# Slot attention and a GELU network on one core: the written order of the first 490 pieces is changed

## The chip, the core and the metric

The kernel runs on one core of a Trainium2 chip. The metric is the device time of one execution in microseconds (us); the number given for a kernel is the median of three runs. PE is the matrix engine (PEld its weight loads), DVE, ACT and POOL are the three engines that work on vectors, and SP only issues transfers (DMA).

## What is computed

```python
a = exp(phi - max(phi, 2));  a = a / (sum(a, 2) + 1e-9)       # softmax over the sequence of 576
k_m, v_m = einsum(a, k), einsum(a, v)                         # 32 slots of 64 per batch and head
scores = q @ k_m.T / 8                                        # 8 batches, 8 heads, 576 x 32
attn = softmax(scores)                                        # over the 32 slots
x = (attn @ v_m).transpose(0, 2, 1, 3).reshape(4608, 512)
h = x @ w_in                                                  # w_in 512 x 2048
g = 0.5 * h * (1 + erf(h / sqrt(2)))
out = g @ w_out                                               # w_out 2048 x 512
```

`w_in` and `w_out` come as 64-bit floats, taken as pairs of 32-bit integers, and are decoded on the chip. Every product is made from a high and a low part of its operands (hi*hi + hi*lo + lo*hi) in the format fp32r.

## The kernel before

The program is one list of **pieces**, small functions such as `h.0.3.1`, that are called one after the other. Each engine gets its instructions in the order of this list and works through them strictly in that order; an instruction starts when its turn has come and its operands and its place in memory are there. Engines run apart from each other and meet only in such waits. The first 1044 pieces stand in a string `START` (line 53 on), which sets their order by hand; what comes later is put in order by due times. A second string, `HOME`, says which buffer each tile uses; a piece that writes into a buffer waits until the last reader of what was in it is done. An ending `:a` or `:d` on a copying piece says that ACT or DVE makes the copy.

The first pieces are the start of everything and so have little to hide behind. They are, with the lines that stand in the profile:

- `Lphi`, `Lkv0`, `Lkv`, `Lq`, `Lwi.f`, `Lwo.f` (lines 372, 412/413, 396, 420/427, 300): transfers of phi, of keys and values, of queries, and of 512 KB each of `w_in` and `w_out`, for f = 0 to 15. All go through SP's one queue.
- Decoding of one half f.k (k = 0 is `w_in`, k = 1 is `w_out`): `dB` two instructions on ACT (lines 321 and 322), `dC`, `dG`, `dS` on DVE (lines 326, 330, 334), then an addition on POOL, `dDi.f` for `w_in` (line 356, out `w_in`) or `dDo.f` for `w_out` (line 356, out `y`). `dE.f` (line 246, out `wo`) and `dF.f` (line 362) split `w_out` into its high and low part.
- Softmax of phi and slots: `amax` (440, DVE), `aexp` (446, ACT), `anorm` (453), `at` (471, PE, transposes, tile pt), `atc` (246, ACT, copies to aT), `slots` (575, PE, tile pk), `km` (593), `slotsT` (604, PE, tile tn), `kT` (246). For batch 0 the keys come first and the values half a stage later, so `slots.0.g.0`, `slotsT.0.0`, `kT.0.0` are the keys and `slots.0.g.1`, `slotsT.0.1`, `kT.0.1` the values.
- Scores of batch 0: `ns.0`, `ns.1` (633, PE, tile psc), `nc` (246, copies sc), `n_score.x` (679, PE), and on DVE and ACT `n_max`, `n_sub`, `n_exp`, `n_sum`, `n_inv`, `n_mul` (698 to 718), for three parts x; back through PE with `n_T.x` (738, tile pT), and split by `n_hi` (753, ACT) and `n_lo` (757, DVE) into p_hi and p_lo. `n_hi.2` and `n_lo.2` hold the last 64 columns, from `n_T.2`. Batch 1 does the same in a whole with `score.1.hf` (633), `sT` (776), `max`, `sub`, `exp`, `sum`, `inv`, `mul`, `pT` (820), `ph`, `pl` for each half hf.
- `Up.b.f.n` (633, PE, tile pu) multiplies the values' slots by `w_in`; `Uh` and `Ul` (246 and 934) split it. It needs the decoded `w_in` f.
- `h.b.f.hf` (979, PE): six matmuls, hi by p_hi, hi by p_lo, lo by p_hi. `gelu.b.f.hf` (1003, 1005, 1006, ACT), `gh` (246) and `gl` (1012, DVE) give the two parts of g.
- `p.b.f` (1025, PE, tile acc): four times three matmuls, gh by wo_hi, gh by wo_lo, gl by wo_hi. Eight steps f of batch 0 are followed by eight of batch 1, then eight and eight again; `o` empties acc after each eight.
- `W` (346): matmuls of ones whose result nobody reads.

On PSUM there are eight banks: four for acc (used before that by the transposes and scores of batch 0), two that h alternates between, and a pair called `at`, with one generation at a time. `pt`, `pk`, `tn`, `psc` and `pu` all take this pair in turn, so each of them waits until the last one has been copied out.

Of the kernel before, what the change touches and what calls it, by code (L numbers as in the profile page):

```python
# [59 lines left out]
Lwi.2 W.3.246 W.3.245 W.3.244 W.3.243 W.3.242 W.3.241 W.3.240 slots.0.0.1 n_sub.1 aexp.1.0  # L60
Lkv.1.0.1 dS.0.0 dE.0:a dS.1.0 dG.0.0 Lkv.1.0.2 W.3.249 W.3.248 W.3.247 slots.0.1.1 dDi.1
km.0.0.1 n_exp.1 Lkv.1.0.4 n_sum.0 amax.1.1 W.3.29 km.0.1.1 Lkv.1.1.2 dDi.0 n_sum.1 aexp.1.1
slotsT.0.1 Lkv.1.1.1 n_inv.0 kT.0.1 Lwi.4 dB.3.1 n_max.2 n_mul.0 W.3.455 W.3.454 W.3.453
W.3.452 W.3.451 W.3.450 Up.0.0.1 dF.0 Uh.0.0:a W.3.456 n_T.0 Lkv.1.0.3 Ul.0.0 dB.2.1 n_inv.1
Up.0.1.1 Lq.1.0 n_mul.1 Uh.0.1:a dC.2.1 Lwi.3 dB.2.0 n_T.1 Ul.0.1 Lkv.1.1.0 dS.2.1 n_sub.2
at.1.0.0 dG.2.1 n_exp.2 n_hi.0 at.1.1.0 dC.2.0 dDo.2 atc.1.0.0:a n_sum.2 n_lo.0 h.0.0.0
atc.1.1.0 n_inv.2 dE.2:a dS.2.0 n_mul.2 n_hi.1 at.1.1.4 at.1.0.4 dG.2.0 n_T.2 atc.1.1.4
atc.1.0.4:a n_hi.2 slots.1.0 dC.3.1 dDi.2 anorm.1 Lkv.1.1.3 n_lo.1 Lkv.1.1.4 n_lo.2 h.0.0.1
gelu.0.0.0 Lphi.2.0 dS.3.1 km.1.0 dG.3.1 Lwo.4 Up.0.2.1 gelu.0.0.1 Lwi.5 dF.2 dB.3.0 dDo.3
h.0.1.0 Lwo.7 Uh.0.2:d Lwo.5 Ul.0.2 h.0.1.1 gh.0.0:a Lphi.2.1 dC.3.0 Lwi.7 slots.1.1 gelu.0.1.1  # L70
gl.0.0 Lwi.6 gelu.0.1.0 dG.3.0 dE.3 h.0.2.0 km.1.1 dS.3.0 gh.0.1:a amax.2.0 dDi.3 dB.4.0
slotsT.1 h.0.2.1 kT.1:d dF.3 dB.4.1 Up.0.3.1 dC.4.0 dG.4.0 p.0.0 Uh.0.3 dB.5.0 gl.0.1 Ul.0.3
gelu.0.2.1 dG.5.0 gelu.0.2.0 dB.5.1 dC.4.1 dS.4.0 score.1.0 dC.5.0 dDi.4 h.0.3.0 Lq.1.1
sT.1.0.1 sT.1.0.0 Lwo.6 h.0.3.1 dS.5.0 dG.4.1 dDi.5 Up.0.4.1 gelu.0.3.1 max.1.0 p.0.1 Uh.0.4:a
gelu.0.3.0 Ul.0.4 sub.1.0 dS.4.1 dC.5.1 exp.1.0 dDo.4 gh.0.2:a sum.1.0 Up.0.5.1 dG.5.1 h.0.4.0
Uh.0.5:a dE.4 gl.0.2 h.0.4.1 gh.0.3:a Ul.0.5 dS.5.1 p.0.2 dF.4 dDo.5 inv.1.0 gelu.0.4.1
amax.2.1 dB.6.0 dC.6.0 mul.1.0 gelu.0.4.0 dE.5 score.1.1 gl.0.3 dB.6.1 h.0.5.0 dS.6.0 dF.5
# [1629 lines left out]
```

## Time and profile before

| | |
|---|---|
| median of three runs | 688.5 us (687.85 to 688.77) |
| the profiled execution: device time | 688.54 us |
| the profiled execution: span of the trace | 686.8 us |
| busy share of the span: PE, PEld, DVE, ACT, POOL | 98%, 85%, 67%, 58%, 7% |
| PE busy | 675.6 us |

The device time is 1.7 us longer than the span of the trace, and 0.04 us from the median. Times below are us from the span's start. In a timeline a row has the start, how long it took, the engine, the line, the operation with out<-in, shapes and count, and in brackets the idle time of this engine just ahead of it and what ended that. Rows of equal instructions are merged.

### The profile page before, as it was taken

To read this page: it belongs to the slowest core of one execution; us is meant where nothing else is said; L and a number is where in the kernel's file an instruction comes from. 1 tells how busy PE (TensorE), PEld (TensorE's weight loads), DVE (VectorE), ACT (ScalarE), POOL (GpSimd) and SP (SyncE) were. 2 spreads that over 40 slices of the span, in tenths; PEclk is the share of its full clock that TensorE was granted. 3 is DMA by queue.
4 is the path that set the end of the run, shared out by engine and by line. 5 is a ranking of instruction groups with operands and counts; after the bars stand their busy time and mean duration, and the time that the engine had idled before them with its cause. 6 is when DMAs were issued, how large, how long until landed. Compare 5 with 4: busy or idle time off the path is not lost.

```text
span 686.8 us, 13988 instructions
## 1 busy us (share of the span) xinstructions
PE 675.6 (98%) x5440; PEld 583.8 (85%) x5440; DVE 463.0 (67%) x912; ACT 396.4 (58%) x977; POOL 45.6 (7%) x38
## 2 busy tenths in 40 slices
...
GB/s 336 368 305 89 122 211 102 82 108 196 54 193 208 175 177 165 67 177 191 266 49 31 154 107 333 284 280 411 64 150 161 66 1 154 158 31 1 33 1 61
DMA packets 54173, 105.11 MB, mean 153 GB/s; under 512 B 5724, under 2 KB 23900, under 8 KB 52572
## 3 DMA queue, kind: packets, MB, share of 16 engines
...
q8 instruction: 43, 0.70, 0.4%
...
## 4 chain that ended last, share of the span: by engine, by line
PE 89%; DMA 4%; DVE 3%; ACT 2%; issue 1%; SPq 0%; DVEq 0%; ACTq 0%
PE acc L1025 31%; PE h L979 28%; PE m L1270 19%; PE pu L633 4%; PE tacc L1025 3%; DMA kv<-kv 1%; DMA raw<-w_in 1%; PE psc L633 1%; PE psc L550 1%; DMA phi<-phiT 1%; DMA q<-qT 1%; DMA raw<-w_out 1%; PE x L550 1%; PE pk L550 0%; DVE gl L1012 0%
## 5 line engine op out<-in xcount | busy, mean ns | idle before, releaser
L979 PE MATMUL h<-p_hi,U 128*128 128x288 f32 x1024 | 203.8, 298 | 0.3 <-ACT p_hi L753 0.3
L1025 PE MATMUL acc<-wo,gh 128*128 128x512 f32 x640 | 198.9, 392 | 0.0
L979 PEld LDWEIGHTS h<-p_hi,U 128*128 128x128 f32 x1024 | 160.9, 188 | 19.4 <-issue 6.0
L1025 PEld LDWEIGHTS acc<-wo,gh 128*128 128x128 f32 x640 | 116.0, 188 | 25.5 <-issue 1.2
L1025 PE MATMUL acc<-wo,gl 128*128 128x512 f32 x320 | 125.1, 391 | 0.2 <-DVE gl L1012 0.2
L979 PE MATMUL h<-p_lo,U 128*128 128x288 f32 x512 | 109.2, 295 | 0.2 <-DVE p_lo L757 0.2
L1212 ACT CAST hi<-x 128x384 fp32r<-128x384 f32 x108 | 61.3, 568 | 37.1 <-DVE x L1205 34.0
L979 PEld LDWEIGHTS h<-p_lo,U 128*128 128x128 f32 x512 | 81.4, 188 | 0.5 <-DVE p_lo L757 0.5
L1270 PE MATMUL m<-wo,hi 128*128 128x256 f32 (+1 forms) x378 | 81.5, 298 | 0.2 <-DVE o L1300 0.2
L997 ACT ACTIVATE gf<-h 128x256 f32<-128x256 f32 x96 | 36.9, 387 | 76.5 <-PE h L979 52.0
L1012 DVE TENSOR_TENSOR gl<-gf,gh 128x512 fp32r<-128x512 f32 x80 | 57.0, 714 | 30.0 <-ACT gh L246 27.5
L1216 DVE TENSOR_TENSOR lo<-x,hi 128x384 fp32r<-128x384 f32 x108 | 67.1, 622 | 12.3 <-ACT hi L1212 12.1
L994 ACT ACTIVATE x<-h 128x256 f32<-128x256 f32 x96 | 36.9, 385 | 63.5 <-PE h L979 63.5
L1025 PEld LDWEIGHTS acc<-wo,gl 128*128 128x128 f32 x320 | 60.1, 188 | 14.1 <-DVE gl L1012 1.1
L1270 PE MATMUL m<-sum,hi 128*128 128x256 f32 x324 | 62.5, 282 | 0.0
L1270 PEld LDWEIGHTS m<-wo,hi 128*128 128x128 f32 x378 | 60.3, 190 | 2.6 <-DVE o L1300 0.5
L1201 DVE TENSOR_TENSOR x<-x 128x256 f32<-128x256 f32 x56 | 23.8, 424 | 57.2 <-ACT x L994 57.2
L1270 PE MATMUL m<-wo,lo 128*128 128x256 f32 x216 | 60.9, 282 | 0.0
L1270 PEld LDWEIGHTS m<-sum,hi 128*128 128x128 f32 x324 | 50.4, 190 | 0.2
L1270 PE MATMUL m<-sum,lo 128*128 128x256 f32 x162 | 45.5, 281 | 0.0
L934 DVE TENSOR_TENSOR U<-pu,U 128x512 fp32r<-128x512 f32 (+2 forms) x38 | 30.8, 827 | 20.9 <-ACT U L246 20.8
L1270 PEld LDWEIGHTS m<-wo,lo 128*128 128x128 f32 x216 | 41.0, 190 | 0.0
...
## 6 DMA issues: line engine op xcount, KB each, us to landing
...
```

The costliest lines, as they stand in the source:

```text
L550: nc.tensor.matmul(pk[32 * j : 32 * j + 32, : 2 * D], st["aT", b][:, c, g, 32 * j : 32 * j + 32], st["kv", b, g, c][:, :, j, :], start=(c ...
L633: nc.tensor.matmul(ps[g][M * j : M * j + M], st["kT", b][rows, t, M * j : M * j + M], moving[j][rows], start=True, stop=True,)
L934: nc.vector.tensor_sub(u[:, ..., 1, :], pu, u[:, ..., 0, :].bitcast(F32))
L979: i = nc.tensor.matmul(h[:, :HS], u[g][w], x[:, g, :], start=(n == 0), stop=(n == 3 * G - 1))
L994: nc.scalar.activation(x, h.rearrange("p (a n) -> p a n", a=2), AF.Gelu)
L997: nc.scalar.activation(gf[:, f % 2 * n : f % 2 * n + n], h, AF.Gelu)
L1012: nc.vector.tensor_tensor(g_of("gl", *k), g_of("gf", *k), g_of("gh", *k).bitcast(F32), op=ALU.subtract)
L1025: nc.tensor.matmul(acc, x, w[:, f, :], start=(first and n == 0), stop=(last and n == 2))
L1201: nc.vector.tensor_tensor(x[:, 5:7], x[:, 1:2].to_broadcast([P, 2, P]), x[:, 0:3:2], op=ALU.subtract)
L1212: nc.scalar.copy(split_of("hi", b, hf, i, part), source(b, hf, i, part))
L1216: nc.vector.tensor_tensor(lo, source(b, hf, i, part), hi.bitcast(F32), op=ALU.subtract)
L1270: nc.tensor.matmul(d, x, y, start=(i == 0 and k == 0 and bank not in seen), stop=(i == NP - 1 and k == len(three) - 1), skip_group_check=True,
```

## The change

Only `START` differs. It holds the same 1044 pieces in both kernels. The order differs up to piece 489; right after it comes `h.0.8.0`, where batch 0's second half begins after eight steps of batch 0 and eight of batch 1, and from there on the lists are the same. 13 copies get another engine: `dE.1`, `kT.1`, `gh.0.6`, `ph.1.1`, `gh.1.2`, `gh.1.3`, `gh.1.4` go from DVE to ACT; `dE.0`, `o.0.0.7`, `gh.1.0`, `gh.1.1`, `gh.1.5`, `dE.11` from ACT to DVE. `aexp.2.1` and `aexp.2.0`, which stood on both sides of `exp.1.1`, stand together much later, after `gh.1.5`; ACT's list therefore has two more loads of a function table (40 instead of 38).

```diff
-Lwo.1 Lphi.0.1 Lphi.0.0 Lkv0.0.0 Lkv0.1.0 Lwo.0 dB.1.1 Lq.0.0 amax.0.1 Lq.0.1 aexp.0.1 amax.0.0
-dC.1.1 dG.1.1 aexp.0.0 anorm.0 at.0.0.0 dS.1.1 dDo.1 at.0.1.0 atc.0.0.0:a at.0.0.4 at.0.1.4
...
+Lphi.0.1 amax.0.1 Lwo.1 dB.1.1 aexp.0.1 Lphi.0.0 dC.1.1 amax.0.0 dS.1.1 dG.1.1 aexp.0.0 anorm.0
+Lwo.0 dB.0.1 dG.0.1 Lkv0.0.0 at.0.1.4 Lkv0.1.0 dC.0.1 dS.0.1 dDo.1 dDo.0 dE.0:d W.4.3 Lq.0.0
...
+gl.0.3 dF.4 Uh.0.5:a sum.1.0 Ul.0.5 inv.1.0 gelu.0.4.1 Lwi.6 dB.6.0 mul.1.0 dE.5 dG.6.0 Lwo.6
+dB.6.1 dF.5 p.0.2 p.0.3 dC.6.0 dS.6.0 Lwo.7 Lq.1.1 pT.1.0 score.1.1 sT.1.1.1 sT.1.1.0 Lwi.7
```

In the last two lines `score.1.1` now stands behind `p.0.2` and `p.0.3`; before it stood between them. On SP's queue the first eight transfers were `Lwo.1`, two of phi, four of keys, `Lwo.0`; now they are phi, `Lwo.1`, phi, `Lwo.0`, four of keys. The ninth and tenth are the two of `Lq.0` in both. Of the later ones `Lwi.3` moves ahead of batch 1's last keys and values and of the queries.

Three places, by engine. On **ACT**, from `kT.0.1` (the first row) to `n_hi.0` (p_hi_0). Before:

```order
L446 ACTIVATE phi_232,sm_373<-phi_232,nm_303 128x576
L246 COPY kT_271<-tn_1_424 128x128
L321 ACTIVATE y_433<-raw_305 128x512
L322 ACTIVATE raw_305<-raw_305 128x512
L246 CAST U_0_455<-pu_0_446 128x2x128
L321 ACTIVATE y_468<-raw_335 128x512
L322 ACTIVATE raw_335<-raw_335 128x512
L246 CAST U_0_455<-pu_1_473 128x2x128
L321 ACTIVATE y_468<-raw_335 128x512
L322 ACTIVATE raw_335<-raw_335 128x512
L710 ACTIVATE s_2_498<-s_2_498 128x256
L753 CAST p_hi_0_508<-pT_0_459 128x288
```

Now (ACT):

```order
L246 COPY kT_271<-tn_1_412 128x128
L321 ACTIVATE y_440<-raw_366 128x512
L322 ACTIVATE raw_366<-raw_366 128x512
L246 CAST U_0_431<-pu_0_422 128x2x128
L321 ACTIVATE y_458<-raw_376 128x512
L322 ACTIVATE raw_376<-raw_376 128x512
L246 CAST U_0_431<-pu_1_463 128x2x128
L446 ACTIVATE phi_286,sm_364<-phi_286,nm_288 128x576
L321 ACTIVATE y_458<-raw_376 128x512
L322 ACTIVATE raw_376<-raw_376 128x512
L753 CAST p_hi_0_495<-pT_0_475 128x288
```

The exponential of batch 1's phi (L446, `aexp.1.1`) has moved from ahead of `kT.0.1` to behind the second U, and `n_exp.2` (L710) has moved behind `n_hi.0`.

On **PE**, the first two steps h of batch 0, with `n_T.2` (out pT_2) and the slots of batch 1 (out pk_0). Before:

```order
L979 MATMUL h_0_0_523<-p_hi_0_508,U_0_455 128x288 x2
L471 MATMUL pt_4_540<-ident,phi_232 64x128 x2
L738 MATMUL pT_2_544<-ident,s_2_498 128x128 x2
L575 MATMUL pk_0_551<-kv_0_0_325,aT_500 32x128 x4
L575 MATMUL pk_0_551<-kv_0_1_375,aT_500 32x128 x4
L575 MATMUL pk_0_551<-kv_0_2_381,aT_500 32x128 x4
L575 MATMUL pk_0_551<-kv_0_3_465,aT_500 32x128 x4
L575 MATMUL pk_0_551<-kv_0_4_410,aT_500 32x128 x4
L979 MATMUL h_1_0_585<-p_hi_1_536,U_0_455 128x288 x2
```

Now (PE):

```order
L979 MATMUL h_0_0_531<-p_hi_0_495,U_0_431 128x288 x2
L471 MATMUL pt_4_538<-ident,phi_286 64x128 x2
L575 MATMUL pk_0_544<-kv_0_0_448,aT_499 32x128 x4
L575 MATMUL pk_0_544<-kv_0_1_472,aT_499 32x128 x4
L575 MATMUL pk_0_544<-kv_0_2_482,aT_499 32x128 x4
L575 MATMUL pk_0_544<-kv_0_3_455,aT_499 32x128 x4
L575 MATMUL pk_0_544<-kv_0_4_401,aT_499 32x128 x4
L738 MATMUL pT_2_567<-ident,s_2_510 128x128 x2
L979 MATMUL h_1_0_583<-p_hi_1_526,U_0_431 128x288 x2
```

The two transposes `n_T.2` have moved from ahead of the slots to behind them, right ahead of the step `h.0.0.1` that reads what becomes of them.

On **DVE**, around the decoding of `w_in` 3 (out y_433 and raw_305 before, y_440 and raw_366 now), from `dF.2` (L362) on. Before:

```order
L362 TENSOR_TENSOR wo<-y_468,wo 128x512
L246 CAST U_0_455<-pu_2_601 128x2x128
L934 TENSOR_TENSOR U_0_455<-pu_2_601,U_0_455 128x2x128
L326 TENSOR_SCALAR y_433<-y_433 128x512
L1012 TENSOR_TENSOR gl_0_667<-gf_0_592,gh_0_638 128x512
L330 TENSOR_SCALAR raw_305<-raw_305 128x512
L334 TENSOR_SCALAR y_433<-y_433 128x512
```

Now (DVE):

```order
L362 TENSOR_TENSOR wo<-y_458,wo 128x512
L246 CAST U_0_431<-pu_2_596 128x2x128
L934 TENSOR_TENSOR U_0_431<-pu_2_596,U_0_431 128x2x128
L330 TENSOR_SCALAR raw_366<-raw_366 128x512
L326 TENSOR_SCALAR y_440<-y_440 128x512
L334 TENSOR_SCALAR y_440<-y_440 128x512
L440 TENSOR_REDUCE nm_663<-phi_581 128x1 x2
L1012 TENSOR_TENSOR gl_0_693<-gf_0_570,gh_0_608 128x512
```

The three steps of `w_in` 3 now stand together, and `gl.0.0` and two reductions behind them.

## Rows read from the trace of the kernel before

**Rows 1.** Stretches, core 0: from:to, length, busy us (count) of engines, clock, DMA.

```profile
10.00:20.00 10.00, 8.08 (x121) 6.09 (x117) 6.97 (x14) 6.35 (x14) 1.29 (x1) 0.83 1.03 397
...
70.00:80.00 10.00, 10.00 (x60) 9.01 (x58) 9.51 (x20) 8.96 (x22) 0.00 (x0) 1.00 0.39 142
```

**Rows 2.** Timeline of PE, 10 to 15 us.

```profile
10.43 0.65 PE L575 MATMUL pk<-kv,aT 128*32 128x64 f32 x32 [0.28 <-DMA kv<-kv]
...
13.03 0.67 PE L633 MATMUL psc_h<-q,kT 64*32 64x256 f32 x16 [0.60 <-DMA q<-q]
14.58 0.77 PE L633 MATMUL psc<-q,kT 64*32 64x320 f32 x16 [0.88 <-DMA q<-q]
```

**Rows 3.** Stretches, PE alone: busy us, granted clock, DMA share, GB/s.

```profile
15.00:16.00 1.00, 1.00 (x19) 0.70 1.06 426
16.00:18.00 2.00, 2.00 (x11) 0.50 1.03 387
18.00:19.00 1.00, 1.00 (x8) 0.60 1.00 372
```

**Rows 4.** Timeline of ACT, 22 to 29 us.

```profile
22.78 0.78 ACT L446 ACTIVATE phi<-phi,nm 128x576 f32<-128x576 f32 x1
...
23.56 0.24 ACT L246 COPY kT<-tn 128x128 f32<-128x128 f32 x1
...
25.86 0.67 ACT L321 ACTIVATE y<-raw 128x512 f32<-128x512 f32 x1 [0.48 <-DVE wo L362]
...
28.50 0.42 ACT L710 ACTIVATE s<-s 128x256 f32<-128x256 f32 x1
28.82 0.68 ACT L753 CAST p_hi<-pT 128x288 fp32r<-128x288 f32 x2
```

**Rows 5.** Timeline of PE, 22 to 34 us.

```profile
22.86 0.33 PE L604 MATMUL tn<-ident,km 128*128 128x128 f32 x1
...
29.25 0.70 PE L979 MATMUL h<-p_hi,U 128*128 128x288 f32 x2 [0.31 <-ACT p_hi L753]
...
31.59 0.44 PE L738 MATMUL pT<-ident,s 128*128 128x128 f32 x2 [0.24 <-DVE s L703]
32.16 1.43 PE L575 MATMUL pk<-kv,aT 128*32 128x128 f32 x40
33.52 0.53 PE L979 MATMUL h<-p_hi,U 128*128 128x288 f32 x2
```

**Rows 6.** Timeline of ACT, 30 to 34 us.

```profile
30.68 0.62 ACT L246 CAST wo<-y 128x512 fp32r<-128x512 f32 x1 [0.21 <-POOL y L356]
...
32.07 0.33 ACT L753 CAST p_hi<-pT 128x64 fp32r<-128x64 f32 x2
32.42 1.28 ACT L1003 ACT_TABLE_LOAD   x1
```

**Rows 7.** Timelines of ACT, POOL and PE, the decoding of w_in 3.

```profile
35.91 0.67 ACT L321 ACTIVATE y<-raw 128x512 f32<-128x512 f32 x1 [0.83 <-DMA raw<-w_in]
...
39.45 1.32 POOL L356 TENSOR_TENSOR w_in<-y,raw 128x512 int32<-128x512 int32 x1 [3.16 <-DVE y L334]
...
40.83 0.45 PE L633 MATMUL pu<-w_in,kT 64*32 64x128 f32 x16 [0.44 <-POOL w_in L356]
```

**Rows 8.** Timeline of PE, the seventh Up of batch 0 (`Up.0.6`).

```profile
60.42 0.45 PE L633 MATMUL pu<-w_in,kT 64*32 64x128 f32 x16 [0.24 <-DVE sT L776]
```

**Rows 9.** Timelines of DVE and PE, where p.0.4 takes gl.0.4.

```profile
60.50 0.69 DVE L1012 TENSOR_TENSOR gl<-gf,gh 128x512 fp32r<-128x512 f32 x1
...
61.37 0.39 PE L1025 MATMUL acc<-wo,gl 128*128 128x512 f32 x1
```

**Rows 10.** Timelines of DVE and POOL, one short operation met by POOL and not.

```profile
25.94 0.17 DVE L717 TENSOR_SCALAR smx<-smx 128x16 f32<-128x16 f32 x1
...
52.70 1.54 POOL L356 TENSOR_TENSOR y<-y,raw 128x512 int32<-128x512 int32 x1 [2.12 <-DVE y L334]
...
52.97 1.30 DVE L808 TENSOR_SCALAR smx<-smx 128x18 f32<-128x18 f32 x1
```

More of the change, by code (lines that the diff above doesn't have):

```diff
@@ L60 @@
[L60 to L77, printed above, removed]
```

60 lines of the change are left out of this document (38 added, 22 removed).

## The prediction, made before the changed kernel was run

> **What bounds the kernel now.** Two questions decide a change of order: where does PE wait, and what does it wait for. The table of stretches answers the first. Between 10 and 20 us PE is busy 8.08 of 10 us, between 70 and 80 us 10.00 of 10 [rows 1]. PE's work is the same in both kernels (the same pieces), and nothing behind `h.0.8.0` changes. So the device time can move only by what PE waits ahead of that point, and by the time lost to a slower clock or to matmuls of ones, whose number is the same. The timelines of PE and of its suppliers answer the second question, and they show three parts. Up to 15 us PE waits for transfers: keys at 10.43, queries at 13.03 and 14.58 [rows 2]. From there to the first step `h.0.0.0` at 29.25 the scores of batch 0 go through DVE and ACT, and the last wait is for ACT's `n_hi.0` [rows 4, 5]. After that PE is nearly full, with a few waits left of which I use two: 0.44 us for the decoded `w_in` 3 [rows 7] and 0.24 us for `sT.1.1` [rows 8]. A microsecond that the first step comes earlier is a microsecond of the total if it arrives at the steps behind, since PE is full after them.
>
> **Part 1: transfers and the decoding of `w_out` 0, no change.** `Lwo.0`, 512 KB, now goes ahead of the keys. At 397 GB/s [rows 1] that is 1.32 us, so the second keys, asked at 10.43, come at about 11.75. In the kernel before, `ns.0` at 13.03 had waited 0.60 us for queries [rows 2], of which some 0.2 us were left after `kT.0.0` was there, so without that wait it stands at 12.8. One of the two `km` now runs ahead of the second slots (0.2 us less), and `ns.0` comes at 12.8 + 1.32 - 0.2 = 13.9, its end (0.67) at 14.6. `ns.1` could not start before 14.58 in any case, as it waited 0.88 us for the tenth transfer [rows 2], which is tenth in both lists with the same bytes ahead of it. The decoding of `w_out` 0 on ACT, two instructions of 0.67 us that overlap by 0.1 [rows 4], 1.2 us together, used to stand between `kT.0.0` and the copies of the scores, where ACT waited for `ns.1` anyway; now it stands ahead of the copies `atc`, where ACT waits for keys. It hides in both places: its cover was the queries, and now is the keys. Bounds: -0.3 (the scores find DVE emptier) to +0.7 (the keys come later still by the difference between transfers). I take 0.
>
> **Part 2: from the values to `n_hi.0`, -0.3 us.** The values' transposes `slotsT.0.1` stand at 22.86 and take 0.33 [rows 5], held by the values' transfers, whose place in the queue moves little (512 KB less one way, two loads swapped). `kT.0.1` could have started at 23.25, and started at 23.56 since `aexp.1.1` was ahead of it on ACT from 22.78 [rows 4]. That one has moved behind the second U. From the start of `kT.0.1` to `n_hi.0` at 28.82 ACT took 5.26 us. Of this the idle 0.48 us goes (it waited for `dF.0`, now done far earlier), `n_exp.2` goes with 28.82 - 28.50 = 0.32, and `aexp.1.1` comes with 23.56 - 22.78 = 0.78 [rows 4]. New: 23.25 + 5.26 - 0.48 - 0.32 + 0.78 = 28.5. `h.0.0.0` would start at 29.25 - 0.3 = 28.9 [rows 5]; PE's own transposes ahead of it end about then too. DVE, which is full there, has `n_mul.1` done near 27 in both lists, as `Ul.0.0` now stands ahead of `n_mul.0` and waits for ACT. Range -0.8 to +0.4.
>
> **Part 3: `n_T.2` behind the slots, +0.3 us, which gives part 2 back.** Before, PE filled the time until the last two copies `atc` were done (32.07, where `n_hi.2` follows them, [rows 6]) with `n_T.2` at 31.59, and had the slots of batch 1 (1.43) at 32.16 and `h.0.0.1` at 33.52 [rows 5]. `n_hi.2` was hidden under the slots. Now the slots come first. On ACT `dE.2` (0.5 us and an idle 0.21 ahead of it, at 30.68 [rows 6]) leaves this stretch and `n_exp.2` (0.32) enters, so that the copies end 0.7 earlier with part 2's 0.3, near 31.4; the slots take until 32.8, `n_T.2` (0.44) until 33.2, `n_hi.2` follows (the table load of 1.28 [rows 6] and the first gelu, now ahead of it, are just through by then), and `h.0.0.1` starts some 0.3 later: 33.5, where it was. Nothing covers this chain of transposes, copy and step, and it costs what part 2 brought. I take 0 for both parts together, with the range -0.6 to +0.7; the slots also need two transfers of values that have moved back in the queue and would land near 31.2, a cover of only some 0.5 us.
>
> **Part 4: the decoded `w_in` 3, -0.44 us.** `Up.0.3` waited 0.44 us at 40.83 for POOL's `dDi.3` at 39.45 (1.32 us), and at its root ACT's first decoding step at 35.91 had waited 0.83 us for the transfer [rows 7]; between them stood `gl.0.0` on DVE. `Lwi.3` now has 0.8 MB less ahead of it in the queue, some 2 us at the measured rate, and the DVE steps stand together ahead of `gl.0.0`. ACT can start near 35.1, DVE ends near 37.6, POOL near 39.0, where PE asks at 40.4. The wait goes with 1.4 us to spare. What is late next: `gl.0.0` for `p.0.0`, which DVE has by 39.8. -0.44 in full, from 0 to -0.44.
>
> **Part 5: `score.1.1` behind `p.0.3`, -0.24 us.** `Up.0.6` waited 0.24 us at 60.42, because DVE's `sT.1.1` still read the pair of banks [rows 8]. Now less DVE work stands ahead of `sT.1.1` and PE has one `p` less between it and the score, so DVE asks for the scores right when they are there. I have it done near 58.8, with `Up.0.6` asked at 59.7. From +0.3 to -0.24; I take -0.24.
>
> **The rest at nothing.** The 13 copies change engine within one list each; on both engines they cost 0.3 to 0.6 us and lie beside PE's steps of 2.7 us. The two added table loads (1.28 each as in [rows 6]) and the two `aexp.2` stand after `gelu.1.5.1`: 4.5 us on ACT, until `gelu.1.6.0` must free a bank for `h.1.7.0`, some 8 us of PE's work later. The cover is 3 us; if it were gone, each microsecond would be lost whole.
>
> **Sum.** 0 + 0 - 0.44 - 0.24 = -0.68. Against the profiled execution, 688.54, that is 687.9; the median of the runs, 688.5, lies 0.04 from it, so the forecast is 687.9.
>
> **Weighing two rules.** POOL's addition of 1.54 us at 52.70 met a short DVE operation at 52.97, which took 1.30 us where its like at 25.94 took 0.17 [rows 10]: it ended with POOL's. The Trainium skill, SBUF — State Buffer, section "Who interferes with whom", says why: DVE and GpSimd share a pair of ports as an exclusive lock, and the later one blocks to the end; so a new order can put a costly step of DVE where a cheap one stood. By the rule one such meeting on PE's path would make the sum 687.9 + 1.1 = 689.0, by the order alone it stays at 687.9; the trace agrees with the rule in this row.
> The granted clock fell to 0.50 (1.2 GHz) from about 15.4 to 18.8 us [rows 3], after a stretch in which PE kept waiting [rows 2]. The Trainium skill, TensorE: Matmul & The Clock Gate, section "HAM oscillation — how this bites in real kernels", says that waits of PE for transfers bring the lower clock back. The trace agrees, with its 0.50. By the rule the longer wait for keys would bring a second stretch (rival E), by the row alone one as before.
>
> **The rivals.**
> A (as summed), 687.9, its own range 687.1 to 688.7: chance 0.45.
> B, the early gain arrives. Decoding `w_out` 0 early takes its 1.2 us [rows 4] out of the score chain after all, since it delayed the copies or DVE behind them, and no part of it is lost in part 3: 688.54 - 1.2 - 0.68 = 686.7. For it: ACT and DVE are full behind the scores. Against: `ns.1` is held by queries, and `kT.0.1` by values. 0.22.
> C, slower: DVE becomes the bound. Place: `gl.0.4`, which was ready at 61.19 for a matmul at 61.37 [rows 9], 0.2 us of slack. About 1.0 us of DVE work leaves its front (`kT.1`, `dC.6.1`, `dS.6.1`), and PE asks 0.68 earlier: 0.5 us of slack now. Every DVE operation that meets POOL loses up to 1.30 - 0.17 = 1.13 [rows 10]; three more of these than before are 3.4, less 0.5, and PE waits 2.9: 690.8. It decides from 0.5 us of lost DVE time on, and is slower beyond the measurement from 2.5. For it: four additions of POOL fall into that stretch. Against: the step hit hardest, `inv.1.0` at 52.97, moves away from POOL. 0.15.
> D, parts 1 and 3 cost: the keys are not covered (+0.7) and the slots wait for values (+0.6): 687.9 + 1.3 = 689.2. 0.13.
> E, a second stretch of the lower clock as long as the first: granted 0.70, 0.50 and 0.60 [rows 3] are 0.6 + 2.0 + 0.8 = 3.4 us at half speed. On full steps it costs half of that: 687.9 + 1.7 = 689.6. For it: PE waits longer between 8 and 11 us now. 0.05.
>
> **How the numbers follow.** A measurement of this kernel tells 0.2%, 1.4 us, from no change: faster is below 687.1, slower above 689.9. Faster: nearly all of B and a little of A, 0.24. Slower: C and a little of D and E, 0.16. The rest 0.60. The range from 686.4 to 690.0 leaves out the lower part of B and most of C.
>
> **What would show it.** Part 1: `ns.1` near 14.6. Part 2: `n_hi.0` near 28.5. Part 3: `n_T.2` near 32.8 and `h.0.0.1` near 33.5. Parts 4 and 5: `Up.0.3` and `Up.0.6` without a wait. PE busy all of 70 to 80 us. The forecast is wrong if `h.0.0.1` is off by more than 0.8 us from 33.5, if PE waits between 42 and 80 us, or if the clock falls a second time.

## The result and the profile after

The changed kernel takes 697.13 us in the median of six runs (694.07 to 700.27), the kernel before 688.45 us (six runs): a ratio of 1.0127, with a 95% interval from 1.0088 to 1.0167. In a second series it was 695.07 us against 688.37, 1.0102 (1.0083 to 1.0121). The change makes the kernel slower by 1.0 to 1.3%, where the forecast had 687.9 us, "no change" as the likeliest outcome (0.60), and 0.16 for slower; the measured time lies above its range, 686.4 to 690.0. The first six runs lie in two groups of three, near 694.4 and near 699.7; the profile is one of the first group (694.27 us, span 692.5 us).

The table follows PE through the two profiles. A place is the start of a piece; between two neighbouring places PE has the same work in both kernels, except that some steps have changed places between `p.0.1` and `p.1.6`.

| place | before, us | after, us | difference |
|---|---|---|---|
| `h.0.0.1` | 33.52 | 34.15 | +0.63 |
| `Up.0.3` | 40.83 | 41.31 | +0.48 |
| `Up.0.6` | 60.42 | 61.34 | +0.92 |
| `p.1.7` | 111.12 | 112.86 | +1.74 |
| `h.0.8.0` (from here on the lists are equal) | 113.84 | 116.19 | +2.35 |
| `h.0.9.0` | 116.53 | 120.68 | +4.15 |
| `p.0.9` | 122.53 | 128.28 | +5.75 |
| end of the span | 686.8 | 692.5 | +5.7 |

So 3.4 of 5.7 us are lost behind the point at which the lists have become equal again, within 12 us. The row of `h.0.9.0` in the kernel before, which had no wait:

```profile
116.53 0.53 PE L979 MATMUL h<-p_hi,U 128*128 128x288 f32 x2
```

First the stretches that answer to [rows 1] and [rows 3] (core 0; from:to, length, busy us (count) of PE, PEld, DVE, ACT and POOL, clock, DMA share, GB/s), in the changed kernel:

```profile
10.00:20.00 10.00, 6.74 (x137) 4.63 (x137) 7.80 (x16) 6.28 (x17) 1.82 (x3) 1.00 1.04 385
70.00:80.00 10.00, 10.00 (x66) 8.04 (x67) 9.67 (x19) 8.47 (x19) 1.31 (x1) 1.00 0.83 316
```

The same for PE alone, around the first scores and around the place of the loss:

```profile
15.00:19.00 4.00, 2.96 (x30) 1.00 1.02 388
117.00:120.00 3.00, 1.95 (x24) 1.00 0.57 150
121.00:122.00 1.00, 1.00 (x9) 0.90 0.35 88
122.00:125.00 3.00, 3.00 (x13) 0.50 0.82 305
125.00:126.00 1.00, 1.00 (x6) 0.89 0.44 180
```

Between 70 and 80 us PE is as full as before. The half clock of [rows 3] is not there in this profile; instead the granted clock is 0.50 (1.2 GHz) around 122 to 125 us, right behind a wait of PE. The timeline of PE shows that wait, and the rows that answer to [rows 5], [rows 7] and [rows 8]:

```profile
29.68 0.69 PE L979 MATMUL h<-p_hi,U 128*128 128x288 f32 x2 [0.30 <-ACT p_hi L753]
...
32.04 1.43 PE L575 MATMUL pk<-kv,aT 128*32 128x128 f32 x40 [0.63 <-ACT aT L246]
...
34.15 0.53 PE L979 MATMUL h<-p_hi,U 128*128 128x288 f32 x2 [0.30 <-ACT p_hi L753]
...
61.34 0.45 PE L633 MATMUL pu<-w_in,kT 64*32 64x128 f32 x16 [0.72 <-DVE sT L776]
...
84.17 0.50 PE L1025 MATMUL acc<-wo,gl 128*128 128x512 f32 x1 [0.53 <-DVE gl L1012]
...
120.68 0.54 PE L979 MATMUL h<-p_hi,U 128*128 128x288 f32 x2 [1.73 <-ACT gf L1003]
```

`h.0.9.0` at 120.68 waits 1.73 us for ACT's `gelu.0.8.0`, which has to free the bank. ACT's timeline says why that one is late:

```profile
110.17 0.62 ACT L246 CAST gh<-gf 128x512 fp32r<-128x512 f32 x1 [1.07 <-PE acc L1025]
114.30 0.68 ACT L321 ACTIVATE y<-raw 128x512 f32<-128x512 f32 x1 [3.51 <-DMA raw<-w_in]
...
116.74 1.28 ACT L446 ACT_TABLE_LOAD   x1
118.03 0.78 ACT L446 ACTIVATE phi<-phi,nm 128x576 f32<-128x576 f32 x1
...
118.92 1.28 ACT L1003 ACT_TABLE_LOAD   x1
120.22 0.41 ACT L1003 ACTIVATE gf<-h 128x288 f32<-128x288 f32 x1
```

ACT stood idle for 3.51 us for the transfer of `w_in` 13, and behind that decoding came `aexp.3.1` with its two table loads, and only then the gelu, at 120.22. In the kernel before it was at 115.67:

```profile
115.67 0.41 ACT L1003 ACTIVATE gf<-h 128x288 f32<-128x288 f32 x1
```

The 0.6 us between `p.1.7` and `h.0.8.0` come from late transfers as well. DVE waited for phi, with `gl.1.7` behind that step, and PE then waited 0.32 us at 113.79 for `gl.1.7`:

```profile
111.82 0.75 DVE L440 TENSOR_REDUCE nm<-phi 128x1 f32<-128x576 f32 x1 [2.04 <-DMA phi<-phiT]
```

Last SP's queue, where each row is the time for which the queue is held by the issue named:

```profile
92.24 13.27 SPq L300 DMA_DIRECT2D raw<-w_in  x2
105.56 0.42 SPq L494 DMA_DIRECT2D row<-nm  x1
106.09 0.37 SPq L372 DMA_DIRECT2D phi<-phiT  x1
106.50 0.43 SPq L300 DMA_DIRECT2D raw<-w_in  x1
106.97 0.43 SPq L300 DMA_DIRECT2D raw<-w_out  x1
```

The first row is `Lwi.12` and `Lwi.14`. `Lwi.14` needs the place of `raw_11`, and waits until 105.18 for POOL to have done with it:

```profile
103.39 1.76 POOL L356 TENSOR_TENSOR y<-y,raw 128x512 int32<-128x512 int32 x1
```

Everything behind it waits too: the store `mw.2` (1 KB, `row<-nm`), `Lphi.3.1`, `Lwi.13` (106.50; before 93.2) and `Lwo.13`. In the kernel before, the three loads stood ahead of `Lwi.14`, so that nobody needed anything behind it:

```profile
92.80 0.33 SPq L300 DMA_DIRECT2D raw<-w_out  x1
93.18 13.14 SPq L300 DMA_DIRECT2D raw<-w_in  x3
106.75 0.33 SPq L494 DMA_DIRECT2D row<-nm  x1
```

### The profile page after: what moved, and what is told of

It is laid out like the page before. It is cut to its first block, busy times and chain, and to the rows that moved or that the text cites. A ratio compares the mean times of both kernels' runs of the same rounds, so it can differ in the third digit from the quotient of the medians.

```text
span 692.5 us, 13994 instructions
## 1 busy us (share of the span) xinstructions
PE 676.6 (98%) x5440; PEld 584.0 (84%) x5440; DVE 471.7 (68%) x911; ACT 399.3 (58%) x980; POOL 46.5 (7%) x38
## 4 chain that ended last, share of the span: by engine, by line
PE 85%; DVE 5%; DMA 4%; ACT 4%; issue 1%; POOL 0%; SPq 0%; ACTq 0%; DVEq 0%; POOLq 0%
PE acc L1025 28%; PE h L979 27%; PE m L1270 19%; PE pu L633 4%; PE tacc L1025 3%; DMA raw<-w_in 2%; DMA raw<-w_out 1%; DVE gl L1012 1%; PE psc L633 1%; PE psc L550 1%; ACT raw L322 1%; DMA phi<-phiT 1%; ACT y L321 1%; PE x L550 1%; DVE wo L362 1%
## 5 line engine op out<-in xcount | busy, mean ns | idle before, releaser
L1012 DVE TENSOR_TENSOR gl<-gf,gh 128x512 fp32r<-128x512 f32 x80 | 59.3, 743 | 31.7 <-ACT gh L246 29.2
```

Of the source, the lines that this page charges most:

```text
L1012: nc.vector.tensor_tensor(g_of("gl", *k), g_of("gf", *k), g_of("gh", *k).bitcast(F32), op=ALU.subtract)
```

## The experiments

The kernels of one table line ran in the same series as their runs of the kernel before. All but e6 and g4 start from the changed list or from a hybrid: the changed list up to `p.0.1` (47 us) and the rest in the order of before (the **head**), or the other way round (the **tail**).

| kernel | us, median (runs) | ratio to before, 95% interval |
|---|---|---|
| after_again: the changed kernel | 695.07 (6) | 1.0102 (1.0083 to 1.0121) |
| e4_head_after: head of the change | 689.87 (12) | 1.0024 (1.0010 to 1.0038) |
| e5_tail_after: tail of the change | 694.23 (6) | 1.0080 (1.0062 to 1.0097) |
| e9_ones_first: ones ahead of the slots | 700.28 (6) | 1.0150 (1.0118 to 1.0181) |
| e1_queue: two pieces in SP's queue | 691.77 (4) | 1.0047 (1.0029 to 1.0065) |
| e2_behind_gelu: decoding 13 behind the gelu | 699.87 (4) | 1.0149 (1.0124 to 1.0173) |
| e3_aexp_early: aexp.2 back | 696.04 (4) | 1.0105 (1.0090 to 1.0120) |
| e6_before_late: before, late loads and amax.3.1 | 692.23 (4) | 1.0046 (1.0031 to 1.0060) |
| f1_lwi14: tail, one load behind | 689.71 (10) | 1.0022 (1.0009 to 1.0034) |
| f2_mw2: tail, one store behind | 689.97 (10) | 1.0021 (1.0009 to 1.0034) |
| f3_lock: f1, DVE away from POOL | 689.68 (10) | 1.0022 (1.0009 to 1.0035) |
| f4_nT2: head, n_T.2 back | 692.60 (9) | 1.0054 (1.0031 to 1.0078) |
| g0_head_again: e4 once more | 689.54 (11) | 1.0028 (1.0008 to 1.0047) |
| g1_more_ones: head, ten ones added | 690.54 (11) | 1.0028 (1.0009 to 1.0047) |
| g3_copies: f1, dF.4 and two copies | 689.60 (11) | 1.0013 (1.0002 to 1.0024) |
| g4_before_plus: before, parts 4 and 5 alone | 691.51 (8) | 1.0047 (1.0031 to 1.0063) |

**Where the loss lies: e4, e5 and the control.** The edits are the two cuts at `p.0.1`.

> Hybrid: the changed list up to p.0.1 (47 us), then the pieces that are left in the order of the kernel before. It holds the moved scores, the early decoding of w_out 0 and parts 1 to 4 of the forecast, but not the late transfers. If the head costs only what its profile of 694.3 shows at p.0.1 (+0.51): 689.0 (688.5 to 690), with, by theory C, some runs 5 us above (693.5 to 695). If the loss of the changed kernel is in the head: above 692 in all runs.

> Hybrid: the list of before up to p.0.1, then the pieces that are left in the changed order, with the late transfers, the two aexp.2 behind gh.1.5 and DVE's work on POOL's additions at 53 and 82 us. By the differences at PE (+5.75 at the end less +0.51 at p.0.1) 693.7 (693 to 694.6), and by theory C one group only, since the first 47 us are those of before. If the tail is harmless: 688.5 to 689.5.

> The changed kernel once more, as the control of this call. Its six runs lay in two groups, near 694.4 and near 699.7 us, with mean granted clocks of 0.994 to 0.997 and 0.988 to 0.990. Theory C (in the group near 699.7 the clock falls to 0.5 for some 10 us from about 21 us on, while the scores of batch 0 wait for each other, after PE has waited 2.2 to 2.5 us for the values at 20 us): two groups again, and a profile near 699 shows that stretch, with h.0.0.0 some 4.4 us later than in the profile of 694.3. Rival: the slower group is something late in the program, and the first 110 us are alike.

Both hybrids came out as the differences on PE had said: 1.0080 for the tail and 1.0024 for the head, together 1.0104, and the changed kernel of the same series is at 1.0102. The tail's six runs reach from 692.9 to 695.5, the head's from 688.3 to 694.0. The control's reach from 693.9 to 697.9, and its profile has not the stretch that theory C names, so it decides nothing on that theory.

**SP's queue: e1, e3, e2 and e6.** Theory Q blames the place of four transfers behind `Lwi.14`, rival T ACT's own load. e1 moves two pieces:

```diff
-Lwi.12 dDo.11 dE.11:d dF.11 Lwi.14 mw.2 p.1.5
+Lwi.12 dDo.11 dE.11:d dF.11 p.1.5
...
-aexp.3.1 Lq.2.0 o.1.2.7:d
+aexp.3.1 Lq.2.0 Lwi.14 mw.2 o.1.2.7:d
```

> The changed kernel with two pieces moved: Lwi.14 and mw.2 (the 1 KB store of the row maxima) stand behind Lphi.3.1, Lwi.13, Lwo.13 and Lq.2.0 in SP's queue instead of ahead of them. Theory Q (SP's queue: these four transfers stand behind Lwi.14, which waits until 105.2 us for POOL, so w_in 13 lands at 114.2, ACT idles 3.5 us and gelu.0.8.0 comes 4 us late): w_in 13 lands before 107, the wait of h.0.9.0 (1.73 us) and the half clock from 121.8 are gone, about 690.6 us (690.0 to 691.3), and no runs near 699. Rival T (ACT's own work: two aexp.2 with two more table loads, 4.2 us, are too much there): no change, 693.5 to 694.5 with others near 699.

691.77 us, 0.5 us above the range given for theory Q. In its profile `w_in` 13 is there at 107.3, and neither the wait of `h.0.9.0` nor the half clock at 122 us is left: from `p.1.7` (+3.19 against before) to `p.0.9` (+3.22) nothing more is lost. What it has too much came earlier: its profile has the head at half clock from 12.1 to 18.9 us, and is at +1.44 at `p.0.1`.

e3 takes ACT's load away instead, and leaves the queue:

```diff
-gh.1.5:d aexp.2.1 aexp.2.0 p.1.4
+gh.1.5:d p.1.4
...
-exp.1.1 gl.0.5
+exp.1.1 aexp.2.1 aexp.2.0 gl.0.5
```

> The changed kernel with aexp.2.1 and aexp.2.0 back right behind exp.1.1, where the exponential's table is loaded anyway: two table loads fewer, and 4.2 us of ACT free at 98.8 us. Theory Q: SP's queue is as before, Lwi.14 still waits for POOL's dDi.11 and dDo.11 and the four transfers behind it: 693 to 694.5, with the runs near 699 still there. Rival T: 690.5, h.0.9.0 without a wait.

696.04 us: no gain, and above the 693 to 694.5 that theory Q gave it, again by a later head (+1.54 at `p.0.1` in its profile, where the values of batch 0 came at 21.21 instead of 20.15 and the clock stayed at 1.00). ACT was still idle for 4.10 us ahead of `dB.13.0` (116.56), since `Lwi.13` was issued at 108.2. Rival T falls.

e2 leaves the transfers late and moves the decoding behind the gelu:

```diff
-dB.13.0 dG.12.1 dDo.12 gl.1.7 p.1.7 Lwo.13 dB.13.1 Ul.0.8 dC.12.0 dS.12.0 aexp.3.1 Lq.2.0
+dG.12.1 dDo.12 gl.1.7 p.1.7 Lwo.13 Ul.0.8 dC.12.0 dS.12.0 Lq.2.0
...
-h.0.8.0 dC.13.1 h.0.8.1 Lwi.15 gelu.0.8.0 dG.13.1
+h.0.8.0 h.0.8.1 Lwi.15 gelu.0.8.0 dB.13.0 dB.13.1 aexp.3.1 dC.13.1 dG.13.1
```

> The changed kernel with four pieces moved: dB.13.0, dB.13.1, aexp.3.1 (ACT) and dC.13.1 (DVE) stand behind gelu.0.8.0 instead of ahead of it; the transfers stay late. Theory Q with ACT's order as the link: gelu.0.8.0 no longer waits for the transfer of w_in 13, h.0.9.0 has no wait of 1.7 us, about 691 us (690.2 to 692), with decoding 13 about 3 us later and some slack for it. If the late transfers hurt by another way (phi for amax.3.1 on DVE, w_in 13 for its Up): 693 to 694.5.

It failed: 699.87 us. `h.0.9.0` did not wait, but the next step did, 4.39 us for the second half of the gelu, which now stood behind the decoding, the exponential and its two table loads, and the clock fell to 0.50 in that wait, from 126.8 to 133.7. Its profile is of a run of 702.29 us, which is 5.6 us late at `p.0.1` already; 6.7 us more are lost between `p.1.7` (+7.28) and `p.0.9` (+13.94). The timeline of PE in e2:

```profile
129.25 0.85 PE L979 MATMUL h<-p_hi,U 128*128 128x288 f32 x2 [4.39 <-ACT tails L1006]
```

So ACT's order is only the carrier: a late transfer blocks whatever stands behind its decoder. e6 puts the late loads into the kernel before, and with them `amax.3.1`, which needs one of them:

```diff
-dF.7 Lphi.3.1 gelu.0.7.1
+dF.7 gelu.0.7.1
...
-dG.12.1 Lwi.14 dE.11:a
+dG.12.1 Lwi.14 Lphi.3.1 Lwi.13 Lwo.13 Lq.2.0 amax.3.1 dE.11:a
```

(the other four pieces leave their old places likewise. In the changed kernel `amax.3.1` stands ahead of `gl.1.7`, here ahead of `gl.1.6`.)

> The kernel before with one part of the change alone: Lphi.3.1, Lwi.13, Lwo.13, Lq.2.0 and amax.3.1 moved behind Lwi.14, nothing else. Theory Q: w_in 13 lands near 111 instead of 97.5, ACT waits for it ahead of gelu.0.8.0: 2 to 4 us slower, 690.5 to 692.5, perhaps with a half clock near 118 and runs 5 us above. Rival T: 688.5 to 689.0, as the transfers still land before they are needed and ACT has 4.2 us less to do.

692.23 us, 3.4 above before, in the range of theory Q, but by another link: PE waited 2.70 us at 113.07 for `gl.1.6` on DVE, which stood behind `amax.3.1`; that had waited 3.71 us for phi. ACT waited for `w_in` 13 as well (2.49 us). The profile loses 3.0 us between `p.1.0` (+1.37) and `p.1.7` (+4.36). In e6 the store `mw.2` stands behind the loads (109.65), and `w_in` 13, issued at 108.21, landed in 5.45 us, where it takes 8.45 in e5 with the store ahead: here the wait behind `Lwi.14` alone was enough, since PE asks for `gl.1.6` at 110.4, and in the changed kernel for `gl.1.7` only at 113.5.

**One piece is enough: f1 and f2.** Both start from the tail hybrid (e5, 694.23 us).

```diff
-Lwi.12 dDo.11 dE.11:d dF.11 Lwi.14 mw.2 p.1.5
+Lwi.12 dDo.11 dE.11:d dF.11 mw.2 p.1.5
...
-aexp.3.1 Lq.2.0 o.1.2.7:d
+aexp.3.1 Lq.2.0 Lwi.14 o.1.2.7:d
```

That is f1; f2 moves `mw.2` there instead, and leaves `Lwi.14`.

> The hybrid of e5_tail_after (list of before up to p.0.1, then the changed order; 694.2 us) with one piece moved: Lwi.14 stands behind Lq.2.0 in SP's queue, so that its wait for POOL until some 105 us holds up nothing else. Theory Q: Lphi.3.1 is asked right after aexp.2.0 (101.5), w_in 13 lands by 106, h.0.9.0 has no wait and the clock no stretch at 122: 690.2 us (689.6 to 691.0). If the 1 KB store mw.2 or ACT's own work were the cause: 693 to 694.5.

> The same hybrid with another single piece moved: mw.2, the store of 1 KB in 128 rows of 8 bytes, stands behind Lq.2.0; Lwi.14 stays ahead and waits as before. In the changed kernel the store was under way for some 3 us and phi and w_in 13 behind it landed 5.7 and 7.7 us after their issue, where 3.0 to 4.0 are usual. If the store is what slows them (theory M): w_in 13 lands near 110, when ACT asks for it (110.8): 690.3 to 691. If only the order behind Lwi.14 counts (Q alone): w_in 13 still near 113 to 114, 693 to 694.5.

Each alone takes 4.3 to 4.5 us away, of the 5.9 us that e5 has above the kernel before. In e5 the wait is the one of the changed kernel. Its rows for SP's queue and for ACT, which asks for `w_in` 13 there:

```profile
106.09 0.43 SPq L300 DMA_DIRECT2D raw<-w_in  x1
...
114.64 0.68 ACT L321 ACTIVATE y<-raw 128x512 f32<-128x512 f32 x1 [4.26 <-DVE y L326]
```

The second row names a step of DVE that in f2 and in the changed kernel comes after this decoding, so it is not what is needed; `w_in` 13 landed at 114.5, 8.45 us behind its issue. f1 as expected: SP's queue in f1 is held by nothing until it comes to `Lphi.3.1`, which waits for `aexp.2.0`:

```profile
92.06 0.43 SPq L494 DMA_DIRECT2D row<-nm  x1
101.08 0.33 SPq L372 DMA_DIRECT2D phi<-phiT  x1
101.53 0.36 SPq L300 DMA_DIRECT2D raw<-w_in  x1
```

f2 is the more telling. SP still waits there until 104.1, and `Lwi.13` is issued at 104.95, only 1.1 us earlier than in e5 (106.09). Yet ACT has it 4.4 us earlier (110.25, where e5 has 114.64). ACT's timeline in f2:

```profile
109.12 0.63 ACT L246 CAST gh<-gf 128x512 fp32r<-128x512 f32 x1 [1.07 <-PE acc L1025]
110.25 0.68 ACT L321 ACTIVATE y<-raw 128x512 f32<-128x512 f32 x1 [0.50 <-DMA raw<-w_in]
```

The difference is the store of 1 KB that goes ahead of the loads in e5. Stretches of e5 (columns as in the first fence):

```profile
107.00:109.00 2.00, 2.00 (x11) 1.69 (x10) 0.63 (x2) 1.70 (x5) 0.00 (x0) 1.00 1.01 290
109.00:111.00 2.00, 2.00 (x10) 1.65 (x10) 0.38 (x2) 0.62 (x1) 0.00 (x0) 1.00 1.06 146
111.00:113.00 2.00, 2.00 (x10) 1.37 (x8) 1.76 (x3) 0.00 (x0) 0.12 (x1) 1.00 0.61 96
```

and of f2, with the same loads and without the store ahead of them:

```profile
107.00:109.00 2.00, 2.00 (x10) 1.65 (x10) 1.26 (x3) 1.05 (x4) 0.00 (x0) 1.00 1.04 390
109.00:111.00 2.00, 2.00 (x11) 1.65 (x10) 2.00 (x4) 1.38 (x3) 0.70 (x1) 1.00 1.00 373
```

Behind the store the DMA engines are as busy (1.06) and move 146 GB/s instead of 373. So in the tail two things together make the loss: the loads stand behind a transfer that waits, and behind one that is tiny and slow. Without the one there is time enough, without the other the loads are quick enough. The Trainium skill, DMA: Bandwidth & Descriptors, section "Rules for kernel authors", has small transfers as mostly overhead and wants them merged. The trace agrees, with a share of 1.06 for 146 GB/s, and shows here that it is also the loads behind the small transfer that pay.

**What is left in the tail: f3 and g3.** f1 still loses 1.45 us between `p.0.1` (-0.37 in its profile) and `p.1.7` (+1.08). Theory L: DVE operations that meet POOL are stretched. Timeline of DVE in the changed kernel, against 0.69 for `dF`, 0.43 for `gh` and 0.69 for `gl` without POOL:

```profile
53.62 1.81 DVE L362 TENSOR_TENSOR wo<-y,wo 128x512 fp32r<-128x512 f32 x1
...
81.19 1.20 DVE L246 CAST gh<-gf 128x512 fp32r<-128x512 f32 x1 [0.26 <-ACT gf L1005]
82.42 1.69 DVE L1012 TENSOR_TENSOR gl<-gf,gh 128x512 fp32r<-128x512 f32 x1
```

f3 is f1 with

```diff
-gl.0.3 dF.4 Uh.0.5:a sum.1.0 Ul.0.5
+gl.0.3 Uh.0.5:a sum.1.0 Ul.0.5 dF.4
...
-o.0.0.7:d dS.9.0 gelu.1.0.0 h.1.1.0 gelu.1.0.1 dS.8.1 dDi.9 gelu.1.1.0
+o.0.0.7:d gelu.1.0.0 h.1.1.0 gelu.1.0.1 gelu.1.1.0
...
-gh.1.0:d gl.1.0 o.0.2.7:a
+gh.1.0:d gl.1.0 dS.9.0 dS.8.1 dDi.9 o.0.2.7:a
```

and `dE.8` behind `gl.1.1`.

> f1_lwi14 with DVE's costly steps moved out of POOL's additions: dF.4 behind sum.1.0 and Ul.0.5 (which keep their length beside POOL), dS.9.0, dS.8.1 and dDi.9 behind gl.1.0, dE.8 behind gl.1.1. Theory L (the +0.75 us at Up.0.6 and the +1.2 us ahead of p.1.0 come from DVE operations stretched beside POOL: dF.4 1.80 for 0.69, gh.1.0 1.22 for 0.43, gl.1.0 1.69 for 0.69): gh.1.0 and gl.1.0 short, the wait of 0.56 us for gl.1.0 gone, the one of 1.03 us for sT.1.1 down to some 0.2: 688.9 us (688.3 to 689.8). If DVE is simply late by its amount of work: 690.2 as f1_lwi14, with the waits as they were.

The first half did what it should: from `p.0.1` to `Up.0.6` f3 loses nothing, where f1 loses 0.70. The second did not: the wait for `gl.1.0` went, POOL's additions then fell on other steps of DVE, and PE waited 0.23 and 0.72 us at 93.86 and 95.11. DVE in f3:

```profile
83.23 0.43 DVE L246 CAST gh<-gf 128x512 fp32r<-128x512 f32 x1 [0.88 <-ACT gf L1005]
83.70 0.69 DVE L1012 TENSOR_TENSOR gl<-gf,gh 128x512 fp32r<-128x512 f32 x1
...
85.27 1.61 DVE L330 TENSOR_SCALAR raw<-raw 128x512 uint16<-128x512 uint16 x1 [0.21 <-ACT raw L322]
86.66 1.51 DVE L246 CAST gh<-gf 128x512 fp32r<-128x512 f32 x1
...
89.48 1.54 DVE L246 CAST wo<-y 128x512 fp32r<-128x512 f32 x1
```

The times of both kernels, f1 and f3, are the same (689.7). f3's profile is of a run of 692.83 us: the list is that of the kernel before up to `p.0.1`, where the profile is 3.0 us late, with the clock at half in three stretches ahead of 38 us, so the old head can lose time to the clock too. g3 keeps the move of `dF.4`, leaves the rest of f3 away, and has

```diff
-gh.1.0:d
+gh.1.0:a
...
-gh.1.1:d
+gh.1.1:a
```

> f1_lwi14 (689.7 us) with dF.4 behind sum.1.0 and Ul.0.5, and the copies gh.1.0 and gh.1.1 back on ACT, where the kernel before has them. Theory L: the wait at Up.0.6 shrinks from 1.00 to 0.3 us, and the wait for gl.1.0 (0.54) goes, as DVE has two copies less (one of them 1.22 us long beside POOL): 688.5 us (688.0 to 689.2). Rival (ACT has no room for the two copies there, or DVE meets POOL with another operation): only the 0.7 us at Up.0.6, 689.0, with a wait for gl or gelu between 82 and 96 us.

689.60 us: the rival's case. From `p.0.1` (-1.27) to `Up.0.6` (-1.29) again nothing is lost, but `p.1.0` now waits 0.55 us for ACT's `gh.1.0`, and at `p.1.7` (-0.19) the list has lost 1.1 us. So 0.7 us of the tail are shown to be `dF.4` beside POOL, in the profiles, while the medians of f1, f3 and g3 do not differ; the 0.7 to 0.8 around 82 us are a stretch where DVE and ACT are both full, and no run here got them back.

**The spread of the head: e9, f4, g0 and g1.** e2's profile, which is the changed kernel up to 110 us, caught the stretch of half clock that theory C names. Stretches of PE in e2:

```profile
20.00:25.00 5.00, 4.45 (x88) 0.60 1.04 355
25.00:30.00 5.00, 4.49 (x33) 0.50 0.97 344
```

The granted clock is 0.50 for 10.2 us from 21.0 on, right behind a wait of 2.47 us for values, and `h.0.0.0` starts at 34.12 instead of 29.68. In the profile of the changed kernel PE waited 2.19 us there, and the clock stayed at 1.00. Of the 4.4 us, 0.4 were there already when the values came (20.55 for 20.15), so that half clock costs 4.0. The length of the wait does not decide: 3.02 us for values in e3, and 2.70 us at 113 us in e6, left the clock at 1.00, while 1.73 us at 120 us in the changed kernel was followed by 0.50. e9 was to take the wait away, with ones that PE has anyway:

```diff
-slots.0.1.1 Lkv0.0.1 W.3.240 W.3.249 n_exp.0
+W.3.240 W.3.249 W.3.248 W.3.247 W.3.29 slots.0.1.1 Lkv0.0.1 n_exp.0
```

> The changed kernel with five pieces of ones (W.3.240, W.3.249, W.3.248, W.3.247, W.3.29, ten matmuls, 1.1 us) moved from behind the values' slots to ahead of slots.0.1.1, where PE waits 2.2 us for the values; nothing else. Theory C: the wait shrinks to some 1.1 us, the clock does not fall at 21 us, all runs lie near 694.4 (693.5 to 695.3), none near 699. Rival (the slower group has another cause, or PE's wait is not what brings the clock down): about as many runs near 699 as in the control.

A clear miss: the wait for the values went, and four of six runs were near 700. Its profile has half clock at 11 to 18, at 25 to 28 and at 35 to 42 us, and PE's busy time between 20 and 25 us, where the ones had stood, is 3.54 us instead of 4.35. g1 adds ten ones and moves none; g0 is its control, the head hybrid again.

```diff
-slots.0.1.1 Lkv0.0.1
+W.3.230 W.3.231 W.3.232 W.3.233 W.3.234 W.3.235 W.3.236 W.3.237 W.3.238 W.3.239 slots.0.1.1 Lkv0.0.1
```

> The hybrid of e4_head_after once more, the control for g1_more_ones in this call: 689.9 us in the median, from 688.3 to some 694, with mean clocks of 0.992 to 0.999.

> The hybrid of e4_head_after with ten matmuls of ones added (none moved) ahead of slots.0.1.1, where PE waits 1.6 to 3 us for the values: 1.1 us of PE's work in a stretch where it is idle, and the ones behind the slots stay. Theory C2 (the changed head leaves PE idle for too much of 15 to 35 us, and the clock falls for it in some runs): median 689.0 to 689.6, all mean clocks at 0.995 or above, no run above 691.5. Rival (the clock falls for what comes behind 20 us, or for nothing that ones change there): the same spread and median as the control of this call, within 0.7 us.

g1's profile has no wait for the values and the clock at 1.00 throughout, but the median is 690.54 against 689.54 of the control. Its five runs with a mean clock of 0.995 or less took 690.9 to 693.7, its six with 0.998 or more 689.5 to 690.5, so the spread is there as before, and goes with the clock. The ratio to the kernel before is the same in both, 1.0028; the medians lie 1.0 apart, more than the 0.7 that the rival allowed. Theory C2 falls: PE's idle time in front of the slots is not what decides it. Why the head is up to 5 us slower in some runs stays open. The half clock is part of it where a profile caught it, and late values are another (21.1 to 21.3 us instead of 20.15 in the profiles of e1, e3 and g0); what sets either off was not found.

f4 puts `n_T.2` back ahead of the slots, in the head hybrid:

```diff
-slots.1.0 dC.3.1 dDi.2 n_T.2 gelu.0.0.0
+n_T.2 slots.1.0 dC.3.1 dDi.2 gelu.0.0.0
```

> The hybrid of e4_head_after (changed list up to p.0.1, then before's; 689.9 us) with n_T.2 back ahead of the slots of batch 1. Part 3 of the forecast (nothing covers the chain n_T.2, n_hi.2, h.0.0.1 behind the slots): from h.0.0.0 to h.0.0.1 4.45 us before the move, 4.0 to 4.1 after it, 689.5 us in the median, which the runs may not tell from 689.9. Rival (the chain is held by n_mul.2 on DVE, not by PE's order): 4.45 as it was, or more, as PE then waits for n_T.2 with the slots behind it.

692.60 us. Its profile is of a run of 694.75 us and has the half clock from 11.4, from 25.0 and from 35.3 us on. There PE waits 1.16 us for DVE's `n_mul.2` with the slots behind it:

```profile
35.78 0.69 PE L738 MATMUL pT<-ident,s 128*128 128x128 f32 x2 [1.16 <-DVE s L703]
36.40 2.52 PE L575 MATMUL pk<-kv,aT 128*32 128x128 f32 x40
```

From `h.0.0.0` to `h.0.0.1` it is 6.9 us there, against 4.47 in the changed kernel and 4.27 before, so this run bears out the rival in it: with the changed order of DVE, `n_T.2` ahead of the slots blocks them; but the slots themselves took 2.52 us instead of 1.43, at half clock for part of it. How much of the 2.7 to 3.1 us that f4 lies above the head's medians (689.87 and 689.54) is this, and how much the clock, its runs do not tell.

**Parts 4 and 5 of the forecast alone, on the kernel before: g4.**

```diff
-Lwi.4 dB.3.1
+Lwi.3 Lwi.4 dB.3.1
...
-gl.0.0 Lwi.6 gelu.0.1.0 dG.3.0 dE.3 h.0.2.0 km.1.1 dS.3.0
+Lwi.6 gelu.0.1.0 dG.3.0 dE.3 h.0.2.0 km.1.1 dS.3.0 gl.0.0
...
-dF.5 p.0.3
+p.0.3
...
-sT.1.1.0 dS.6.1
+sT.1.1.0 dF.5 dS.6.1
```

> The kernel before with parts 4 and 5 of the forecast by themselves: Lwi.3 ahead of Lwi.4 in SP's queue and gl.0.0 behind dS.3.0 on DVE (part 4), dF.5 behind sT.1.1 on DVE (part 5). By the forecast -0.44 and -0.24: 687.8 us (687.3 to 688.4), Up.0.3 and Up.0.6 without a wait. If what is late next takes their place (gl.0.0 for p.0.0, gl.0.4 for p.0.4): 688.4 as before, with a wait there.

691.51 us, 3.2 slower than before. Both waits that it aimed at are gone, and each came back elsewhere. `Lwi.3` ahead pushed the values of batch 1 back, and the slots waited 0.64 us for them at 33.53. `dF.5` behind `sT.1.1` held `dB.7.1` on ACT, which writes into the place that `dF.5` reads (`y_5` and `y_7` share `wy1`): 60.36 instead of 57.76, and with it the gelu and the copies behind. Timeline of PE in g4:

```profile
64.69 1.09 PE L633 MATMUL pu<-w_in,kT 64*32 64x512 f32 x16 [0.87 <-DVE U L934]
...
67.66 0.51 PE L1025 MATMUL acc<-wo,gl 128*128 128x512 f32 x1 [0.42 <-DVE gl L1012]
```

No version here is faster than the kernel before.

## Why the prediction was wrong, step by step

**The frame.** "The device time can move only by what PE waits ahead of that point" (`h.0.8.0`), and by the clock, was the step that failed. The lists are equal behind that point, but the engines do not arrive there equal: ACT was 4.55 us late with `gelu.0.8.0` (120.22 to 115.67), and SP's queue was late for it. Of 5.75 us, 3.4 fell behind the point, 1.8 as a wait and 1.6 with the half clock that followed; the same queue cost 0.6 just ahead of it, through phi and `gl.1.7`.

**"The rest at nothing."** The two `aexp.2` and their table loads were followed on ACT alone, and there they did hide: `h.1.7.0` does not wait. What the step left out is what it asks of every moved piece, the queues it is moved past. `Lphi.3.1` needs `aexp.2` to be done, `Lwi.13`, `Lwo.13` and `Lq.2.0` had moved with it behind `Lwi.14` and `mw.2`, and SP waits in order. f1 and f2 price that at 4.3 to 4.5 us. Whether the 13 copies were free, g3 could not show: with two of them put back, the time stayed. The "4.5 us on ACT" were 4.24 (98.77 to 103.01), so that size was right; what was missed is the queue.

**Part 1** held: `ns.0` at 13.54 and `ns.1` at 14.41 (forecast 13.9 and 14.6). **Part 2** was mis-sized by 0.75: `n_hi.0` came at 29.25 and not at 28.5, as `slotsT.0.1` started at 23.61 (22.86 before) and `kT.0.1` at 23.92, and the copies U and the second half of the decoding waited once more. **Part 3** was right in its mechanism: the slots at 32.04, then `n_T.2` at 33.41 (forecast 32.8) and the chain that nothing covers, `h.0.0.1` at 34.15 (forecast 33.5, with 0.8 allowed). **Part 4** came true as far as it went: `Up.0.3` does not wait. The head as a whole was forecast at -0.44 at `Up.0.3` and is at +0.48, and e4 and g0 show +1.2 to +1.5 us in the median of their runs.

**Part 5** had the wrong sign: `sT.1.1` was to be done at 58.8, and starts at 60.35, so `Up.0.6` waits 0.72 us instead of 0.24. The cause is the lock of [rows 10] on `dF.4`, 1.81 us for 0.69, as f3 and g3 show. That was rival C with another victim: its place (`gl.0.4`) was wrong, the kind of loss right, its price of 2.9 us too high. With the stretch around 82 us the tail has 1.45 us of it, of which 0.7 are shown.

**Rival E** happened, in another place and for another reason. The forecast looked for a second half clock where keys are waited for, at 10 us, and paid 1.7 for it; it came behind the late gelu at 122 us and cost 1.6. The Trainium skill, TensorE: Matmul & The Clock Gate, section "HAM oscillation — how this bites in real kernels", has waits of PE bring the lower clock. At 122 us the trace agrees; at 20 us, with waits of 2.19 and 2.47 us in the changed kernel and in e2, whose lists are the same up to 110 us, the clock stayed once and fell once, and behind the 3.02 us of e3 it stayed.

**"PE busy all of 70 to 80 us"** came true and said nothing, since the loss was later than any place that the forecast had set for itself to look at.
